# A planner in the kernel sets every engine's order; the first two batches' softmax works on the allowed columns only

## The chip, the core and the metric

The kernel runs on one NeuronCore of a Trainium2 chip. Five engines work side by side, each through its own queue in order: TensorE (PE, with PEld for its weight loads), VectorE (DVE), ScalarE (ACT), GpSimd (POOL) and SyncE (SP), which here issues all transfers between HBM and the on-chip memory. The metric is the time of one execution in microseconds (us), less is better; the time shown is the median of three runs.

## What is computed

```python
# q, k, v: (8 batches, 8 heads, 576 positions, 64) float32
scores = q @ k.T / 8                          # per batch and head
mask_local   = (rel >= 0) & (rel < 32)        # heads 0..3;  rel = query - key
mask_strided = (rel >= 0) & (key % 32 == query % 32)   # heads 4..7
attn = softmax(where(mask, scores, -1e9));  y = attn @ v
x = y as (4608 tokens, 512)
h = x @ w_in                                  # 512 -> 2048, weights in float64
g = h * clip(h + 3, 0, 6) / 6
out = g @ w_out                               # 2048 -> 512
```

Each query sees at most 32 keys (local heads) or 18 keys (strided heads).

## The kernel before

**Attention.** The unit is a pair of heads, 4 pairs per batch, 32 in all; pairs 0 and 1 of a batch are local, 2 and 3 strided. A pair's steps (`pair_steps`, L265) are: load q and k (L240, four DMAs each, 72 KB per DMA) and v (L251, L258, L262); turn q and k by DVE transposes (L289, L293, L301); scores on PE (`s_step`, L320); softmax (`softmax`, L196); turn the probabilities (`p_blocks`, L366, DVE; or `p_whole`, L392, PE and a copy, for the first five pairs); the product with v (`v_step`, L402, tile pv); and the two halves of x, high part by ACT (L428) and rest by DVE (L429). A head is cut into 6 blocks of 96 queries by 128 keys (local) or 5 of 126 by 126 (strided), so a block holds far more columns than its queries may see. Scores of pairs 0 to 7 (batches 0 and 1) are one float32 product (L333); from pair 8 on q and k are each split in a high and a rest part and the product runs in fp32r (L335). Softmax takes the blocks one by one: mask and row minimum in one DVE instruction with its accumulator read (L206), exponent and sum in one ACT instruction with its accumulator read (L211), the division on POOL (L361).

**FFN.** 512 tokens of a batch are one pass of 16 chunks (fc). Per chunk: 12 matmuls of 128x512 into ph (L512 to L514, three per 128 rows of x: weights and x are both in two fp32r parts); then a chain of four instructions, relu on ACT (L539), gate on DVE (L540), high part gh on ACT and rest gl on POOL (L101, L102); then 12 matmuls into four acc banks, two with gh and one with gl (L495, L496, L497). The last 64 positions of each batch are collected over four batches and make a pass of 256 tokens (phl, accl), run after batches 2 and 7.

**Weights.** 32 parts of 512 KB come as float64 bit patterns (L115). A conversion (`conv`, L117) takes three ACT, two DVE (L124, L126) and one POOL instruction per part.

**The order.** While the FFN of batch b runs, the attention of batch b + 1 is issued between its chunks. The first two batches follow a hand-written string ORDER; the later ones a fixed sequence spread over the chunks. The tile framework's scheduler then moves instructions on each engine by its own simulated times and priorities. The first two chunks of batch 0 are started early, 128 rows of x at a time (`mm1_early`, L516).

Of the kernel before, what the change touches and what calls it, by code (L numbers as in the profile page):

```python
# [1 line left out]

# [8 lines left out]
I32 = mybir.dt.int32  # L11
# [10 lines left out]
QB = 96  # L22
NPOS = 18
# [4 lines left out]
WA = 6  # L28
NB = 3
VB = 1  # L30
PLAIN = 8
EC = 2
KP = 4
HP = 100
EV = 11
EARLY = 5
ORDER = "l w q0 t0 q1 v0 t1 a0 b0 v1 q2 l a1 v2 b1 q3 p0 t2 o0 l a2 b2 p1 t3 o1 l a3 v3 w l b3 p2 o2 w q4 w m0 p3 l m1 m2 o3 m3 v4 | q5 t4 a4 b4 v5 t5 q6 p4 o4 a5 l q7 b5 t6 p5 o5 a6 b6 q8 v6 p6 v7 o6 t7 a7 b7 t8 p7 l q9 o7 v8 v9"
DENSE = 8
RATE = 0.95
UB = 3  # L40
AHEAD = 6
# [3 lines left out]
def attention_ffn(ctx: ExitStack, tc, q, k, v, w_in, w_out, out):  # L45
# [7 lines left out]
    LEFT = S - TOK  # L53
    SCALE = 1.0 / float(D) ** 0.5

    const = ctx.enter_context(tc.tile_pool(name="const", bufs=1))
    wp = ctx.enter_context(tc.tile_pool(name="wp", bufs=1))
    xp = ctx.enter_context(tc.tile_pool(name="xp", bufs=2))
    gp = ctx.enter_context(tc.tile_pool(name="gp", bufs=2))
    up = ctx.enter_context(tc.tile_pool(name="up", bufs=UB))  # L60
    ap = ctx.enter_context(tc.tile_pool(name="ap", bufs=1))
    sp = ctx.enter_context(tc.tile_pool(name="sp", bufs=3))
    pacc = ctx.enter_context(tc.tile_pool(name="pacc", bufs=1, space=PSUM))
    pwk = ctx.enter_context(tc.tile_pool(name="pwk", bufs=4, space=PSUM))


    ident = const.tile([P, P], F32, name="ident")
    make_identity(nc, ident)
    three = const.tile([P, 1], F32, name="three")
    nc.vector.memset(three, 3.0)  # L70


    mloc = const.tile([QB, P], F32, name="mloc")
    nc.gpsimd.memset(mloc, 0.0)
    nc.gpsimd.affine_select(
        out=mloc, in_=mloc, compare_op=ALU.is_ge, fill=NEG,
        base=PAD, pattern=[[-1, P]], channel_multiplier=1)
    nc.gpsimd.affine_select(
        out=mloc, in_=mloc, compare_op=ALU.is_ge, fill=NEG,
        base=STRIDE - 1 - PAD, pattern=[[1, P]], channel_multiplier=-1)  # L80
    mstr = const.tile([SB, SB], F32, name="mstr")
    nc.gpsimd.memset(mstr, 0.0)
    mstr3 = mstr.rearrange("p (r m) -> p r m", r=RB)
    nc.gpsimd.affine_select(
        out=mstr3, in_=mstr3, compare_op=ALU.is_ge, fill=NEG,
        base=0, pattern=[[-NPOS, RB], [-1, NPOS]], channel_multiplier=1)
    nc.gpsimd.affine_select(
        out=mstr3, in_=mstr3, compare_op=ALU.is_ge, fill=NEG,
        base=NPOS - 1, pattern=[[NPOS, RB], [0, NPOS]], channel_multiplier=-1)
# [3 lines left out]

    NQ = 4
    FQ = NFC // NQ
    wts = {}

    def split(src, hi, lo, eng):  # L100
        nc.scalar.copy(hi, src)  # L101
        eng.tensor_tensor(out=lo, in0=src, in1=hi.bitcast(F32), op=ALU.subtract)  # L102

    def weight_steps():

        parts = [(w, g, i) for g in range(NQ) for w in "io" for i in range(4)]
        raws = {}

        def load(w, g, i):
# [4 lines left out]
            t = raws[w, g, i] = wp.tile([P, TOK, 2], I32, tag=f"w{w}{g}{i}", name=f"raw{w}{g}{i}")  # L114
            nc.sync.dma_start(t, src.bitcast(I32).rearrange("p (n t) -> p n t", t=2))  # L115

        def conv(w, g, i):  # L117
            raw = raws[w, g, i]
            f = up.tile([P, TOK], I32, tag="u", name=f"f{w}{g}{i}")
            r = raw.rearrange("p n t -> p (n t)")[:, :TOK]  # L120
            nc.scalar.activation(f.bitcast(F32), raw[:, :, 1].bitcast(F32), AF.Copy, scale=2.0 ** -112)
# [501 lines left out]
```

## Time and profile before

| | us |
|---|---|
| median of three runs (lowest, highest) | 1003.33 (1002.16, 1006.83) |
| the profiled execution | 1004.04 |
| its span, first to last instruction | 1002.3 |
| PE busy in it | 950.4 (95%) |
| DVE, ACT, POOL busy | 623.8, 507.1, 408.1 |
| HBM read, written | 46.84 MB, 9.44 MB |
| mean granted TensorE clock | 0.975 of full |

The span falls into stages by the matmuls: attention of batch 0 and the first FFN chunks up to 66.3 us (the first acc matmul), FFN of batch 0 beside attention of batch 1 up to 178.7, six stages of one FFN pass beside one batch of attention, the short pass for the left-over tokens at 389.8 to 439.9, FFN of batch 7 with no attention beside it, and a second short pass at the end. A busy PE is not PE at its peak: matmuls overlap, and when the granted clock is 0.5 each takes twice as long.

### The profile page before, as it was taken

The page shows a single profiled execution, that of the slowest core. Times are in us where ns is not written, and L with a number is a line of the kernel's source. Part 1 is how long each engine was busy: PE and PEld are TensorE (multiplying, and loading weights), DVE is VectorE, ACT ScalarE, POOL GpSimd, SP SyncE. Part 2 cuts the span into 40 slices and gives each one's busy share as a digit, 9 for nine tenths or more (in the row PEclk, how much of TensorE's full clock was granted, in tenths as well). Part 3 has the DMA queues.
Part 4 walks back from the last instruction along what each step waited for, and adds up shares of the span by engine and source line. Part 5 has one row for each costly group of instructions (what it writes and reads, how often), then busy time and mean ns, then how long its engine had stood idle before and what let it go on. Part 6 is the DMA issues. An engine that isn't in the chain of part 4 may idle for free. (4 is left out here: it accounts for less than half of the span.)

```text
span 1002.3 us, 14999 instructions
## 1 busy us (share of the span) xinstructions
PE 950.4 (95%) x4848; PEld 767.8 (77%) x4848; DVE 623.8 (62%) x1837; ACT 507.1 (51%) x1378; POOL 408.1 (41%) x381
## 2 busy tenths in 40 slices
PE   5789897999999999999999999999899999999997
PEld 4667675887787778988787777777778888788896
DVE  7677988677767775136877767776766766211111
ACT  5778676545555534345454544464455544322232
POOL 4446656443444434234443433443344433222221
PEclk8799997999999999999999999999899999999999
DMA  7699601212132222002222211222213110100010
GB/s 150 148 282 281 137 13 27 67 31 47 26 81 39 37 37 61 22 19 43 37 38 60 61 33 35 46 67 39 37 26 81 31 22 14 43 1 1 1 43 21
DMA packets 207085, 57.25 MB, mean 57 GB/s; under 512 B 198304, under 2 KB 198304, under 8 KB 207008
## 3 DMA queue, kind: packets, MB, share of 16 engines
q1 hardware_dynamic: 207008, 56.31, 24.9%
q8 instruction: 38, 0.62, 0.3%
q14 instruction: 39, 0.32, 0.1%
HBM read 46.84 MB, written 9.44 MB: 56 GB/s over the span
## 5 line engine op out<-in xcount | busy, mean ns | idle before, releaser
L102 POOL TENSOR_TENSOR gl<-u,gh 128x512 fp32r<-128x512 f32 x128 | 168.5, 1318 | 255.7 <-ACT gh L101 226.9
L512 PE MATMUL ph<-xh,wi 128*128 128x512 f32 x512 | 207.1, 405 | 5.9 <-ACT wi L101 4.0
L495 PE MATMUL acc<-wo,gh 128*128 128x512 f32 x512 | 203.1, 397 | 1.2 <-ACT gh L101 1.1
L513 PE MATMUL ph<-xl,wi 128*128 128x512 f32 x512 | 203.2, 397 | 0.1
L514 PE MATMUL ph<-xh,wi 128*128 128x512 f32 x512 | 202.1, 396 | 0.0
L496 PE MATMUL acc<-wo,gh 128*128 128x512 f32 x512 | 201.3, 393 | 0.0
L211 ACT ACTIVATE e<-e,st 126x126 f32<-126x126 f32 (+2 forms) x352 | 137.3, 392 | 79.0 <-DVE st L206 77.4
L101 ACT CAST gh<-u 128x512 fp32r<-128x512 f32 x128 | 79.2, 619 | 163.6 <-DVE u L540 143.2
L497 PE MATMUL acc<-wo,gl 128*128 128x512 f32 x512 | 161.0, 397 | 0.0
L540 DVE SCALAR_TENSOR_TENSOR u<-u,ph 128x512 f32<-128x512 f32 x128 | 86.4, 675 | 104.9 <-ACT u L539 104.1
L361 POOL TENSOR_TENSOR e<-e,st 96x96 f32<-96x96 f32 (+1 forms) x96 | 92.9, 981 | 116.7 <-DVE st L358 94.3
L539 ACT ACTIVATE u<-ph,three 128x512 f32<-128x512 f32 x128 | 87.2, 682 | 92.8 <-PE ph L514 88.1
L512 PEld LDWEIGHTS ph<-xh,wi 128*128 128x128 f32 x512 | 97.3, 190 | 31.5 <-ACT wi L101 5.0
L514 PEld LDWEIGHTS ph<-xh,wi 128*128 128x128 f32 x512 | 97.8, 191 | 21.9 <-issue 0.2
L495 PEld LDWEIGHTS acc<-wo,gh 128*128 128x128 f32 x512 | 96.8, 189 | 22.4 <-ACT gh L101 2.2
L513 PEld LDWEIGHTS ph<-xl,wi 128*128 128x128 f32 x512 | 97.8, 191 | 18.5 <-DVE xl L429 0.6
L497 PEld LDWEIGHTS acc<-wo,gl 128*128 128x128 f32 x512 | 95.9, 190 | 20.5 <-issue 0.2
L496 PEld LDWEIGHTS acc<-wo,gh 128*128 128x128 f32 x512 | 96.7, 189 | 18.2
L386 DVE STREAM_TRANSPOSE atstr<-e 32x160 f32<-32x160 f32 x196 | 65.6, 335 | 10.7 <-POOL e L361 8.1
L386 DVE STREAM_TRANSPOSE atloc<-e 32x160 f32<-32x160 f32 (+1 forms) x156 | 56.6, 363 | 16.3 <-POOL e L361 14.3
L206 DVE CUSTOM_DVE_ANT_0 e<-ps,e 96x128 f32<-96x128 f32 (+2 forms) x264 | 65.0, 280 | 2.3
L211 ACT ACTIVATION_READ_ACCUMULATOR e<-e,st 96x1 f32 (+1 forms) x352 | 66.2, 188 | 0.0
(176 smaller groups left out, 1359.1 us busy)
## 6 DMA issues: line engine op xcount, KB each, us to landing
qn<-in_q_dram SPq DMA_DIRECT2D x128, 72.0 KB
kn<-in_k_dram SPq DMA_DIRECT2D x128, 72.0 KB
rawi<-in_moe_w_in_dram SPq DMA_DIRECT2D x16, 512.0 KB
rawo<-in_moe_w_out_dram SPq DMA_DIRECT2D x16, 512.0 KB
out_dram<-ob SPq DMA_DIRECT2D x32, 256.0 KB
vt<-in_v_dram SPq DMA_DIRECT2D x32, 160.0 KB
vt<-in_v_dram SPq DMA_DIRECT2D x160, 31.5 KB
out_dram<-obl SPq DMA_DIRECT2D x8, 128.0 KB
```

The lines of the kernel that those rows point to most:

```text
L102: eng.tensor_tensor(out=lo, in0=src, in1=hi.bitcast(F32), op=ALU.subtract)
L211: nc.scalar.activation(e[:, u, c], e[:, u, c], AF.Exp, bias=mn[:, u:u + 1], scale=-1.0, accum_out=sm[:, u:u + 1])
L361: nc.gpsimd.tensor_tensor(out=x, in0=x, in1=sm[:, bl].unsqueeze(2).to_broadcast(x.shape), op=ALU.mult)
L386: nc.vector.transpose(at[ks, i0:, qs], e[qs, i0:, ks])
L495: nc.tensor.matmul(acc[i], gh[:, sl], woh, start=fc == 0, stop=False)
L496: nc.tensor.matmul(acc[i], gh[:, sl], wol, start=False, stop=False)
L497: nc.tensor.matmul(acc[i], gl[:, sl], woh, start=False, stop=last)
L512: nc.tensor.matmul(ph, wih, xh[:, c], start=c == 0, stop=False)
L513: nc.tensor.matmul(ph, wih, xl[:, c], start=False, stop=False)
L514: nc.tensor.matmul(ph, wil, xh[:, c], start=False, stop=c == NCC - 1)
L539: nc.scalar.activation(u, ph, AF.Relu, bias=three)
L540: nc.vector.scalar_tensor_tensor(out=u, in0=u, scalar=6.0, in1=ph, op0=ALU.min, op1=ALU.mult)
```

## The change

The kernel is written anew around a list planner in it (`Plan`). Every step is an `op` with an engine (or a choice of two), a duration written in the code, what it reads and writes, and a due time; PSUM banks are slots that an op takes and gives back. `emit` walks a simulated time: of the ops whose inputs are there it takes the one that can start first, by due time where several can, and at the end writes all ops in order of their planned start. The framework's scheduler is off (`manual_schedule`), so this is each engine's order. What is computed stays the same. The parts:

- **Batches 0 and 1** (`kept_pair`): scores stay one float32 product, local heads in the same 6 blocks, strided heads in 8 blocks of 128 by 72. ACT copies only the columns that a query may see (64 of 128 for local, 18 of 72 for strided) out of PSUM, in 3 or 4 strips of 32 rows per four blocks. Then, once per head: mask on POOL, maximum on DVE, subtraction on POOL, exponent on ACT, sum on DVE, reciprocal on DVE, product on POOL. All probabilities are turned by DVE (6 strips of 32x192 per local head, 4 of 32x256 per strided head); the PE transposes and their copies go.
- **From batch 2 on** (`pair`): the same instructions as before, whole blocks and split scores, with pv of a pair in one run.
- **PSUM**: four acc banks, two ph banks and two score banks, instead of four acc and four shared. The output tiles use x's memory.
- **Weights**: relu with a slope (Prelu) keeps the sign in the first ACT instruction, so that one DVE instruction (join) takes the place of two.
- **Order of pairs** 0, 2, 1, 3 (and 2, 3, 0, 1 in batch 1).

```diff
-EC = 2
-ORDER = "l w q0 t0 q1 v0 t1 a0 b0 v1 q2 l a1 v2 b1 q3 p0 t2 o0 l a2 b2 p1 t3 o1 l a3 v3 w l b3 p2 o2 w q4 w m0 p3 l m1 m2 o3 m3 v4 | q5 t4 a4 b4 v5 t5 q6 p4 o4 a5 l q7 b5 t6 p5 o5 a6 b6 q8 v6 p6 v7 o6 t7 a7 b7 t8 p7 l q9 o7 v8 v9"
+AHEAD = 27.0
+T0 = 50.0
+TILE = 101.0
+HOP = 0.12
+FETCH = 2.2
...
+    def emit(self):
...
+                    t = max(t0, avail[n])
...
+                    if first is None or (t, due, n) < first:
+                        first = (t, due, n)
...
+            free[e] = end = t + (us() if callable(us) else us)
+            if after:
+                end = dma = max(end + FETCH, dma) + after
...
+        for _, _, n, e in sorted(order):
...
-        def conv(w, g, i):
...
-            nc.vector.scalar_tensor_tensor(out=r, in0=f, scalar=3, in1=r,
...
-            nc.vector.scalar_tensor_tensor(out=f, in0=f, scalar=-2147483648, in1=r,
...
+        def high():
+            f = new(xp, fkey, [P, TOK], I32, f"f{name}")
+            nc.scalar.activation(f.bitcast(F32), tiles[key][:, :, 1].bitcast(F32), AF.Prelu, scale=2.0 ** -112, alpha=2.0 ** 32)
...
+        def join():
+            f = tiles[fkey]
+            nc.vector.scalar_tensor_tensor(out=f, in0=f, scalar=3, in1=bits(),
                                            op0=ALU.logical_shift_left, op1=ALU.bitwise_or)
...
+        op("SP", 0.1, load, writes=[key], due=-2 + 0.1 * k if k < 16 else due - 20.0, early=7.0 if k < 16 else due - 30.0, after=1.7)
+        op("ACT", 0.68, high, reads=[key], writes=[fkey], due=due - 5, room=LATE)
+        op("ACT", 0.68, low, writes=[key], due=due - 5)
+        op("DVE", 0.95, join, reads=[key], writes=[fkey], due=due - 3)
+        op("ACT", 0.63, hi, reads=[fkey], writes=[key], due=due - 2)
+        op("POOL", 1.4, lo, reads=[fkey, key], writes=[key + ("lo",), key], due=due - 1)
...
-    def softmax(ps, mask, skip, e, mn, sm):
...
-            nc.vector.tensor_tensor_reduce(
-                out=e[:, u, c], in0=ps[:, u, 0, c], in1=m[:, u, c], scale=-SCALE, scalar=BIG,
...
-            nc.scalar.activation(e[:, u, c], e[:, u, c], AF.Exp, bias=mn[:, u:u + 1], scale=-1.0,
...
+    def timing(g):
+        b = g // NPAIR
+        if not b:
+            return T0 - 6.0 * (NPAIR - g)
+        return wanted[b] - 6.0 - (NPAIR - 1 - g % NPAIR) * (wanted[b] - opens[b]) / NPAIR
...
+    def kept_pair(g):
+        b, c = divmod(g, NPAIR)
+        c = TURNS[b][c]
...
+            op("SP", 0.25, load, writes=[nkey], due=-60 + 2 * g + (x == "k") if early else due - 35, early=0 if early else due - 45, after=1.9)
...
+                rows = v[b, h0 + j].rearrange("(m t i) d -> i m t d", t=8, i=4)
+                for i in range(4):
+                    nc.sync.dma_start(tiles[vkey][PAD * i:PAD * i + NPOS, j], rows[i])
+        op("SP", 0.2 if loc else 0.4, load_v, writes=[vkey], due=-59.5 + 2 * g if early else due - 30, early=0 if early else due - 35, after=1.7)
...
+                        if e == "ACT":
+                            nc.scalar.copy(to, src)
...
+            def masked(j=j):
...
+                    nc.gpsimd.tensor_tensor(out=e_of(j), in0=e_of(j), in1=m.unsqueeze(1).to_broadcast([n, nblk, w]), op=ALU.add)
...
+                nc.vector.tensor_reduce(out=st_of(j, 0), in_=e_of(j), axis=AX.X, op=ALU.max)
...
+                nc.gpsimd.tensor_tensor(out=x, in0=x, in1=st_of(j, 0).unsqueeze(2).to_broadcast(x.shape), op=ALU.subtract)
...
+                nc.scalar.activation(e_of(j), e_of(j), AF.Exp, scale=SCALE)
...
+                nc.vector.tensor_reduce(out=st_of(j, 1), in_=e_of(j), axis=AX.X, op=ALU.add)
...
+                nc.gpsimd.tensor_tensor(out=x, in0=x, in1=st_of(j, 1).unsqueeze(2).to_broadcast(x.shape), op=ALU.mult)
...
+                op("DVE", 6 * 0.37 if loc else 4 * 0.435, tr, reads=[ekeys[j]], writes=[akeys[j]], due=due - 2 + j)
...
+    def pair(g):
...
+            op("SP", 0.25, load, writes=[nkey], due=due - 38, early=due - 45, after=1.9)
...
-        if b * NPAIR + c >= EARLY:
-            pv = [p_blocks(0), p_blocks(1)] + [v_step(g) for g in groups]
...
-    def mm1_early(c):
-        for fc in range(EC):
-            if c == 0:
-                early[fc] = pwk.tile([P, TOK], F32, tag="w", name=f"ph0_{fc}")
-            mm1(early[fc], fc, c, *xs[0])
...
+                    nc.tensor.matmul(acc, gh, woh, start=fc == 0, stop=False)
+                    nc.tensor.matmul(acc, gh, wol, start=False, stop=False)
+                    nc.tensor.matmul(acc, gl, woh, start=False, stop=end)
+                op("PE", 0.683, mm, reads=list(gk) + wkeys, writes=[("acc", i)],
+                   due=s0 + (fc + 1.5 + i * 0.12) * chunk, mode="f")
...
+                op("PE", 0.683 if n == TOK else 0.36, mm1, reads=xkeys(c) + wkeys, writes=[pk],
+                   due=s0 + (fc + c * 0.12) * chunk, mode="f")
...
+    with tc.manual_schedule():
+        plan.emit()
```

**SP, the start of the program, before.** In a name such as qn0_2 the digits are batch and pair; rawi and rawo are weight parts (group and part). The queue begins so:

```order
L115 DMA rawi00_109<-in_moe_w_in_dram 128x1024
L240 DMA qn0_0_119<-in_q_dram 32x18x32 x4
L240 DMA kn0_0_124<-in_k_dram 32x18x32 x4
L240 DMA qn0_1_139<-in_q_dram 32x18x32 x4
L240 DMA kn0_1_144<-in_k_dram 32x18x32 x4
L251 DMA vt0_0_149<-in_v_dram 96x2x64
L258 DMA vt0_0_149<-in_v_dram 128x5x64 x2
L251 DMA vt0_1_213<-in_v_dram 96x2x64
L258 DMA vt0_1_213<-in_v_dram 128x5x64 x2
L240 DMA qn0_2_218<-in_q_dram 32x18x32 x4
```

And now, from the eighth row on (the first seven are the q and k of pairs 0, 2, 1 and the q of pair 3):

```order
L343 DMA kn0_3_172<-in_k_dram 32x18x32 x4
L347 DMA v0_0_163<-in_v_dram 96x2x64
L352 DMA v0_0_163<-in_v_dram 128x5x64 x2
L460 DMA v0_2_182<-in_v_dram 18x8x64 x8
L347 DMA v0_1_186<-in_v_dram 96x2x64
L352 DMA v0_1_186<-in_v_dram 128x5x64 x2
L460 DMA v0_3_190<-in_v_dram 18x8x64 x8
L273 DMA rawi00_237<-in_moe_w_in_dram 128x1024
L273 DMA rawi01_239<-in_moe_w_in_dram 128x1024
```

The first weight part has moved from row 1 to row 15, behind all q, k and v of batch 0; 15 more weight parts follow it, and then q, k and v of pair 2 of batch 1, which before came behind five weight parts (pair 0 there).

**DVE, ahead of the first gate, before.** st is a head's sums, fo and rawo a weight part, xl the rest of x, u the FFN's gate; pv0_30 is batch 0, pair 3:

```order
L124 SCALAR_TENSOR_TENSOR rawo02_657<-fo02_699,rawo02_657 128x512
L429 TENSOR_TENSOR xl0_108<-pv0_30_605,xh0_107 128x28x16
L429 TENSOR_TENSOR xl0_108<-pv0_34_637,xh0_107 128x4x16
L126 SCALAR_TENSOR_TENSOR fo02_699<-fo02_699,rawo02_657 128x512
L206 ISA e1_01_778,st1_01_780<-ps1_014_815,mloc_89 96x128
```

And now, rows 69 to 79 of DVE (row 84 is the last part of x of pair 3, rows 86 and 87 turn q and k of pair 3 of batch 1, row 88 is the first gate):

```order
L584 STREAM_TRANSPOSE atkept_188<-e0_93 32x8x32 x4
L550 TENSOR_REDUCE st0_3_509<-e1_110 128x8
L440 STREAM_TRANSPOSE qt1_2_349<-qn1_2_373 128x18x32
L553 TENSOR_SCALAR st0_3_509<-st0_3_509 128x8
L554 RECIPROCAL st0_3_509<-st0_3_509 128x8
L381 TENSOR_TENSOR x0_11_678<-pv0_10_623,x0_10_677 128x512
L381 TENSOR_TENSOR left1_1_80<-pv0_11_624,left0_1_79 128x64
L584 STREAM_TRANSPOSE atkept_188<-e1_110 32x8x32 x4
L440 STREAM_TRANSPOSE kplain_118<-kn1_2_383 128x18x32
L289 SCALAR_TENSOR_TENSOR fo03_646<-fo03_646,rawo03_256 128x512
L289 SCALAR_TENSOR_TENSOR fi10_663<-fi10_663,rawi10_258 128x512
```

The transposes of batch 1's pair 2, which need transfers that stand behind 16 weight parts on SP, now stand ahead of the x of batch 0's pairs 1 and 3.

**PE, FFN of batch 7, before.** acc7_0 is acc bank 0 of batch 7, gh7_6 and gl7_6 the two parts of chunk 6:

```order
L513 MATMUL ph7_8_8590<-xl7_7354,wi21_1157 128x512
L495 MATMUL acc7_0_8362<-wo12_1027,gh7_6_8540 128x512
L496 MATMUL acc7_0_8362<-wo12_1027,gh7_6_8540 128x512
L495 MATMUL acc7_1_8363<-wo12_1027,gh7_6_8540 128x512
L496 MATMUL acc7_1_8363<-wo12_1027,gh7_6_8540 128x512
L495 MATMUL acc7_2_8364<-wo12_1027,gh7_6_8540 128x512
L496 MATMUL acc7_2_8364<-wo12_1027,gh7_6_8540 128x512
L497 MATMUL acc7_0_8362<-wo12_1027,gl7_6_8541 128x512
L497 MATMUL acc7_1_8363<-wo12_1027,gl7_6_8541 128x512
```

And now:

```order
L877 MATMUL acc7_0_8384<-wo13_1132,gh7_7_8592 128x512
L878 MATMUL acc7_0_8384<-wo13_1132,gh7_7_8592 128x512
L879 MATMUL acc7_0_8384<-wo13_1132,gl7_7_8597 128x512
L920 MATMUL ph7_8_8567<-x7_30_8189,wi23_1233 128x512
L921 MATMUL ph7_8_8567<-x7_31_8190,wi23_1233 128x512
L922 MATMUL ph7_8_8567<-x7_30_8189,wi23_1233 128x512
L877 MATMUL acc7_1_8390<-wo13_1132,gh7_7_8592 128x512
```

The rest part gl is now needed by the third matmul of a chunk and not the seventh. From the last ph matmul of a chunk to the first acc matmul that needs its gh, PE has 29 other matmuls in the list before (chunk 7) and 18 now (chunk 8).

More of the change, by code (lines that the diff above doesn't have):

```diff
@@ L1 @@
+import heapq
 from contextlib import ExitStack
+from functools import partial
 import concourse.bass as bass
@@ L98, in attention_ffn, with identity @@
[L98 to L109, printed above, removed]
+    left = [[[const.tile([P, HALF * LEFT], F32R, name=f"left{i}_{c}") for i in range(2)]]
+            for c in range(NCC)]
+    def identity():
+        nc.vector.memset(three, 3.0)
+        make_identity(nc, new(const, ("ident",), [P, P], F32, "ident"))
```

1126 lines of the change are left out of this document (704 added, 422 removed).

## The prediction

> **What bounds the kernel now.** I read the page first: the busy time of TensorE, the rows of 40 slices (25.06 us each) for PE, its granted clock and the transfer rate.
>
> ```profile
> PE 950.4 (95%) x4848; PEld 767.8 (77%) x4848; DVE 623.8 (62%) x1837; ACT 507.1 (51%) x1378; POOL 408.1 (41%) x381
> PE   5789897999999999999999999999899999999997
> PEclk8799997999999999999999999999899999999999
> GB/s 150 148 282 281 137 13 27 67 31 47 26 81 39 37 37 61 22 19 43 37 38 60 61 33 35 46 67 39 37 26 81 31 22 14 43 1 1 1 43 21
> ```
>
> PE is the bound: 950.4 of 1002.3 us. What isn't 9 lies in the first seven slices; there the weights come in (282 GB/s in slices 3 and 4). So I cut the span into stages at the matmuls that begin each FFN pass. Columns: window, its us, busy us (instructions) of PE, PEld, DVE, ACT, POOL, granted clock, DMA share, GB/s.
>
> ```profile
> 0.00:66.30 66.30, 48.20 (x296) 38.27 (x296) 47.51 (x182) 47.01 (x166) 29.72 (x52) 0.87 0.79 176
> 66.30:178.70 112.40, 100.33 (x469) 74.17 (x470) 95.79 (x210) 79.29 (x185) 69.73 (x57) 0.92 0.50 130
> 178.70:389.80 211.10, 204.25 (x1017) 164.08 (x1016) 153.92 (x464) 108.16 (x304) 90.34 (x76) 0.99 0.22 45
> 389.80:439.90 50.10, 50.10 (x322) 44.90 (x321) 7.85 (x19) 17.18 (x39) 12.53 (x17) 1.00 0.09 30
> 439.90:754.40 314.50, 305.36 (x1518) 245.46 (x1517) 229.84 (x699) 161.60 (x457) 132.41 (x113) 0.98 0.22 44
> 754.40:857.10 102.70, 102.70 (x521) 82.67 (x520) 67.80 (x226) 51.70 (x149) 40.52 (x36) 1.00 0.15 34
> 857.10:945.50 88.40, 88.40 (x401) 73.07 (x401) 12.49 (x20) 24.14 (x40) 20.59 (x16) 1.00 0.03 12
> 945.50:1002.30 56.80, 51.05 (x313) 45.18 (x312) 8.55 (x19) 18.04 (x39) 12.28 (x16) 0.97 0.09 28
> ```
>
> Three things stand here. The opening takes 66.3 us before the first acc matmul. The second stage has 12.1 us without PE and a clock of 0.92. The six stages of one FFN pass and one batch of attention (windows three, five and six) take 211.1 + 314.5 + 102.7 = 628.3, 104.7 each, while the best of them takes 102.7 with PE never idle. Batch 7 without attention takes 88.4, so attention costs a good stage 14.3.
>
> For the opening I asked what PE waits for (us in total, times, longest), and when the first gate and the first acc matmul come (third field: first and last start).
>
> ```profile
> PE ps L333 <- DVE kplain L293: 9.7, 2, 9.1
> L540 DVE SCALAR_TENSOR_TENSOR u<-u,ph x128: 636/684/691, 63.3 to 946.5; 128x512 f32<-128x512 f32 x128
> L495 PE MATMUL acc<-wo,gh x512: 387/389/796, 66.3 to 952.1; 128*128 128x512 f32 x171
> ```
>
> PE starts on the first q and k, and the first chunk ends with the gate at 63.3; acc follows 3.0 later.
>
> **The opening: transfers.** SP's timeline (start, duration), and the window in which transfers were fastest:
>
> ```profile
> 1.20 2.04 SPq L240 DMA_DIRECT2D qn<-in_q_dram  x4
> 3.28 2.92 SPq L240 DMA_DIRECT2D kn<-in_k_dram  x4
> 10.57 0.50 SPq L251 DMA_DIRECT2D vt<-in_v_dram  x1
> 11.11 1.02 SPq L258 DMA_DIRECT2D vt<-in_v_dram  x2
> 19.36 8.19 SPq L262 DMA_DIRECT2D vt<-in_v_dram  x10
> 78.00:86.00 8.00, 7.76 (x41) 5.72 (x39) 6.84 (x9) 6.37 (x12) 4.42 (x4) 1.00 0.99 372
> ```
>
> Now eight groups of q and k go first: SP is busy with one for 2.04 to 2.92, say 2.25, so 18 us from 1.2 on. Then four v: two local at 0.50 + 1.02, two strided of eight DMAs at 0.82 (8.19 for ten), together 16.2; a DMA now moves less, and at 0.65 (an estimate between the 0.50 of L251 and 0.82) it is 13.4. The weights begin at 32.6. Sixteen parts of 512 KB at the page's 282 GB/s take 1.86 each, 29.8 in all; at the best rate of the trace, 372 GB/s with the DMA engines 99% busy, 22.5. So q of batch 1's pair 2, the next in line, lands between 55 and 62, and k behind it: 56 to 64.
>
> **The opening: DVE.** Its rows by shape (busy, mean ns, then idle before):
>
> ```profile
> L289 DVE STREAM_TRANSPOSE qplain<-qn 128x576 f32<-128x576 f32 x8 | 8.1, 1014 | 2.6 <-DMA qn<-in_q_dram 2.6
> L386 DVE STREAM_TRANSPOSE atloc<-e 32x192 f32<-32x192 f32 x130 | 48.1, 370 | 2.0
> L124 DVE SCALAR_TENSOR_TENSOR rawi<-fi,rawi 128x512 int32<-128x512 int32 x16 | 12.0, 751 | 8.4 <-ACT rawi L122 8.3
> L126 DVE SCALAR_TENSOR_TENSOR fi<-fi,rawi 128x512 int32<-128x512 int32 x16 | 17.0, 1061 | 0.3
> L202 DVE TENSOR_TENSOR e<-ps,mloc 96x256 f32<-96x256 f32 x72 | 29.0, 418 | 32.2 <-PE ps L335 31.4
> L357 DVE TENSOR_SCALAR st<-st 96x6 f32<-96x6 f32 x32 | 13.3, 414 | 5.0 <-ACT e L211 4.7
> L358 DVE RECIPROCAL st<-st 96x6 f32<-96x6 f32 x32 | 5.6, 174 | 0.5
> L429 DVE TENSOR_TENSOR xl<-pv,xh 128x448 fp32r<-128x448 f32 x16 | 16.2, 1013 | 18.7 <-ACT xh L428 18.5
> ```
>
> Ahead of the first gate DVE now has: 8 turns of q and k at 1.01 (8.1), 24 local turns at 0.370 (8.9), 16 strided ones a third wider, 0.49 as an estimate (7.9), 11 joins at 0.75 (8.3), 16 reduces, which the trace does not have, by the nearest row 0.42 (6.7; from 0.17 to 1.01 each), 8 sums and reciprocals at 0.59 (4.7), four rests of x at 1.16 by L429's length (4.6), and four turns of batch 1's q and k at 1.01 (4.0): 53 us of 72. DVE's sum alone doesn't set the time, but its order does: the turns of batch 1's pair 2 stand ahead of the x of pairs 1 and 3, so x, ph and the gate wait for a transfer behind sixteen weights. Landing at 62, two turns (2), then 8 of joins, turns and x that stand between: first gate 72 (70 to 74; with fast transfers 65), first acc 75. The same wait holds up the four instructions of each chunk behind it. So the opening is about 9 longer, although it loses all probability transposes on PE.
>
> **Second stage.** Its 112.4 are 12.1 idle and 100.3 busy at clock 0.92, so 92.3 at full clock. Since the softmax works on six tenths fewer columns (384 and 144 per head instead of 768 and 630), I take half of the idle away (bounds: all, none) and give the clock back, as slow clocks stand in the first slices only, next to idle ones. The extra score and pv blocks (8 instead of 5 per strided head, 24 matmuls) cost nothing by streamed columns and 4.1 by this row's busy time (0.17 each); I take 1.5.
>
> ```profile
> L333 PE MATMUL ps<-kplain,qplain 64*126 64x126 f32 x40 | 6.7, 292 | 0.9 <-DVE st L206 0.9
> ```
>
> 92.3 + 1.5 + 6 = 99.8. Batch 1 then begins at 75 + 99.8 = 174.8 against 178.7: −3.9. Bounds: 160 (fast transfers, no idle) and 190 (a clock of 0.92 and all idle kept).
>
> **The joins.** One DVE instruction replaces two per part, some 1.0 less of DVE for each of 32 parts, on no path after batch 0. What it costs beside POOL:
>
> ```profile
> 105.93 3.63 DVE L126 SCALAR_TENSOR_TENSOR fi<-fi,rawi 128x512 int32<-128x512 int32 x1
> 106.49 1.27 POOL L102 TENSOR_TENSOR wi<-fi,wi 128x512 fp32r<-128x512 f32 x1
> 107.72 1.28 POOL L102 TENSOR_TENSOR gl<-u,gh 128x512 fp32r<-128x512 f32 x1
> ```
>
> A join that starts while POOL goes from one instruction to the next took 3.63, not 0.75. [...] With L126's mean of 1.06 instead of 0.75 the eleven joins cost 3.4 more and the sum would be 980.
>
> **Six stages.** Matmuls are the same, FFN and attention. The planner has PE's work in one list, with pv of a pair in one run, where before its matmuls came in pieces between FFN groups:
>
> ```profile
> 754.40:857.10 102.70, 7.43 (x88) 5.66 (x88) 1.00 0.15 34
> 857.10:945.50 88.40, 1.20 (x16) 1.05 (x16) 1.00 0.03 12
> ```
>
> These are L412's matmuls in the best stage and in batch 7, 84 and 75 ns each. Grouping saves between nothing and about 3.2; I take 1.7, a quarter of the 7.43. So 101.0 per stage, bounds 99.5 and 104.7 (no better than the mean before): 6 x 101 = 606, −22.3. ACT, DVE and POOL are 39 to 73% busy in these stages, so their work stays under PE. The short passes (50.1, 56.8) and batch 7 (88.4) have the same work and hardly any idle: nothing.
>
> **Sum.** 1004.04 − 3.9 − 22.3 = 977.8 for an execution like the profiled one; that lies 0.7 above the median, so 977.
>
> **Rivals.** *B: the opening as short as planned.* If SP's issues and the weights overlap better than my chain (372 GB/s and no turn held up), the first acc comes at about 59, batch 1 at 159, −16 more: 961. For it: the DMA share is 0.79 in the opening, not 1. Against: one queue, 20 us of it for q and k.
>
> *C: the stages don't shrink.* The planner's durations are constants; an engine that runs late against them makes PE wait in queue order, with no other work to take. The gain of 22.3 then fails: 999. For it: 2.7 of an average stage before were idle, waits that the new order needn't remove.
>
> *D: slower.* PE's list now leaves 18 matmuls (4.1 us) from a chunk's last ph to the first acc that needs it, 29 (6.7 us) before, and wants gl two matmuls after gh, six before. The chain is
>
> ```profile
> L539 ACT ACTIVATE u<-ph,three 128x512 f32<-128x512 f32 x128 | 87.2, 682 | 92.8 <-PE ph L514 88.1
> L540 DVE SCALAR_TENSOR_TENSOR u<-u,ph 128x512 f32<-128x512 f32 x128 | 86.4, 675 | 104.9 <-ACT u L539 104.1
> L101 ACT CAST gh<-u 128x512 fp32r<-128x512 f32 x128 | 79.2, 619 | 163.6 <-DVE u L540 143.2
> L102 POOL TENSOR_TENSOR gl<-u,gh 128x512 fp32r<-128x512 f32 x128 | 168.5, 1318 | 255.7 <-ACT gh L101 226.9
> L361 POOL TENSOR_TENSOR e<-e,st 96x640 f32<-96x640 f32 x32 | 41.0, 1282 | 0.0
> ```
>
> 0.682 + 0.675 + 0.619 + 1.318 = 3.29 up to gl, and 20 matmuls at 0.230 (88.4 over 16 x 24) are 4.6, so 1.3 is left, 3.8 before; a softmax product of 1.28 on POOL just ahead of gl, or an attention instruction on ACT or DVE, is enough to stop PE. There are 16 x 7 = 112 such chunks. A stop of 0.24 per chunk on average eats the 26 of gain; at 0.4, 1022. Against it: the planner knows these lengths and places the softmax where the chain leaves room.
>
> *E: POOL holds the joins.* Eleven joins ahead of the first gate, next to POOL's mask, subtract and product passes (three per head now, against one), at 2 us instead of 0.75 (between 0.75 and 3.63) cost 13.8 more. Batch 1 begins at 188: 1004.04 + 9.9 − 22.3, 991. The row of 3.63 speaks for it, the mean of 0.75 against. [...]
>
> **How the numbers follow.** The forecast has a chance of 0.52, B 0.14, C 0.10, D 0.11, E 0.13. This kernel can be told from no change at about 0.5%, 5 us: faster is below 998.3, slower above 1008.3. Faster: forecast 0.50, B 0.14, E 0.11, C 0.03, in all 0.78. No change: forecast 0.02, E 0.02, C 0.06, D 0.02, 0.12. Slower: C 0.01, D 0.09, 0.10. The range takes in C at 999 and half a stage's doubt around it, up to 1003, and goes down to both unknowns at their low end (batch 1 at 160, stages of 99.5: 1004 − 18.7 − 31.3, 954), 955; what it leaves out is D and little of C.
>
> **What would show it.** Right: first gate at 70 to 74 behind a DVE turn of batch 1 that waits for its transfer; batch 1 at about 175; stages of 101 with PE at 100%; short passes unchanged. Wrong: first acc below 62 (B), stages of 104 or more (C), waits of acc for gl or gh in the hundreds (D), joins with a mean of 2 us in the opening (E).

## The result and the profile after

The changed kernel takes 971.98 us (median of four runs, 971.58 to 972.17); the kernel before takes 1004.55 in the same series, the ratio is 0.968, 95% interval 0.965 to 0.970. The forecast was 977, range 955 to 1003. The profiled execution took 971.58 with a span of 969.8, 32.5 less than the span before.

The page's first rows:

```profile
PE 926.3 (96%) x4952; PEld 762.8 (79%) x4952; DVE 604.1 (62%) x1651; ACT 524.2 (54%) x1330; POOL 429.2 (44%) x420
PE   5489999999999999999999999999999999999997
PEclk9978999999999999999999999999999999999999
GB/s 119 235 201 205 141 112 17 84 26 53 35 66 56 45 38 52 45 22 67 17 38 25 82 41 39 41 82 41 39 41 68 56 14 1 44 1 0 21 25 22
```

PE's gaps are gone everywhere but in the first three slices and the last. The clock row needs care: the trace has no record of the clock before 56.2 us, and the 9 of the first two slices only says that none is there. The spacing of the matmuls shows half clock from the first one at 8.3 up to 56.2 (0.43 between the starts of equal ones, 0.23 at full clock; the last section has the lines). So the 0.90 in the first line below is too high: of the opening's 84.9 us, 56.2 (with the 8.3 ahead of the first matmul), 10.3 and 6.8 count as half clock, which leaves 0.57. In the kernel before the same holds only up to 12.7 us, 3.6 after its first matmul.

The stages, cut at the same matmuls as before (first acc, first ph of batch 1, first ph of batch 7; columns as in the prediction):

```profile
0.00:84.90 84.90, 53.90 (x301) 44.58 (x302) 59.75 (x128) 49.36 (x134) 44.03 (x77) 0.90 0.67 180
84.90:177.70 92.80, 92.64 (x498) 73.43 (x497) 62.39 (x116) 67.70 (x143) 62.90 (x61) 1.00 0.38 104
177.70:826.30 648.60, 641.60 (x3464) 527.94 (x3463) 462.42 (x1373) 366.63 (x978) 289.31 (x251) 1.00 0.22 45
826.30:911.30 85.00, 85.00 (x376) 70.38 (x375) 11.01 (x16) 23.14 (x36) 19.55 (x16) 1.00 0.03 13
```

The third line answers to this one of before, six stages and the short pass between them:

```profile
178.70:857.10 678.40, 662.40 (x3373) 537.11 (x3372) 459.42 (x1407) 338.64 (x949) 275.80 (x242) 0.99 0.20 42
```

The two first stages together became 1.0 shorter (178.7 to 177.7; forecast 3.9): the opening is 18.6 longer and the second stage 19.6 shorter, with hardly any idle and a full clock. The six stages with the short pass became 29.8 shorter (forecast 22.3), and what follows them 1.7 (145.2 to 143.5; forecast nothing). In the six stages PE's idle time went from 16.0 (678.40 − 662.40) to 7.0.

The opening shows a wait that the kernel before did not have. ScalarE and VectorE of the changed kernel (start, duration, in brackets the idle time before it):

```profile
38.43 0.66 ACT L281 ACTIVATE fi<-rawi 128x512 f32<-128x512 f32 x1 [10.03 <-DMA rawi<-in_moe_w_in_dram]
40.63 0.90 DVE L289 SCALAR_TENSOR_TENSOR fi<-fi,rawi 128x512 int32<-128x512 int32 x1 [9.29 <-ACT rawi L285]
63.59 1.19 DVE L440 STREAM_TRANSPOSE qt<-qn 128x576 f32<-128x576 f32 x1
77.38 0.68 DVE L932 SCALAR_TENSOR_TENSOR u<-u,ph 128x512 f32<-128x512 f32 x1
```

ScalarE stood 10.0 on the first weight part with softmax copies queued behind it; VectorE stood 9.3 behind ScalarE. The turn of batch 1's q, which the prediction named as the wait, began at 63.59 with no wait at all; the first gate came at 77.4, not 72. From 63.4 to 84.9 the chain that ended last runs through PE, but for 2.2 us, and 13.3 of these 21.5 us are at half clock (up to 69.9, and 76.7 to 83.5). At the spacing of full clock, 0.23 instead of 0.43, that would be some 6 less (an estimate from these rows). The first weight was late because of what the prediction summed up on SP:

```profile
19.63 6.71 SPq L460 DMA_DIRECT2D v<-in_v_dram  x8
28.02 6.44 SPq L460 DMA_DIRECT2D v<-in_v_dram  x8
34.50 1.89 SPq L273 DMA_DIRECT2D rawi<-in_moe_w_in_dram  x4
```

The weights began at 34.5 (forecast 32.6).

### The profile page after: what moved, and what is told of

It is laid out like the page before. It is cut to its first block, busy times and chain, and to the rows that moved or that the text cites. A ratio compares the mean times of both kernels' runs of the same rounds, so it can differ in the third digit from the quotient of the medians.

```text
span 969.8 us, 15040 instructions
## 1 busy us (share of the span) xinstructions
PE 926.3 (96%) x4952; PEld 762.8 (79%) x4952; DVE 604.1 (62%) x1651; ACT 524.2 (54%) x1330; POOL 429.2 (44%) x420
## 4 chain that ended last, share of the span: by engine, by line
PE 77%; DVE 10%; ACT 4%; issue 3%; SPq 3%; DMA 2%; POOL 1%; POOLq 0%; DVEq 0%; ACTq 0%
PE ph L920 11%; PE ph L921 10%; PE ph L922 10%; PE acc L877 10%; PE acc L879 10%; PE acc L878 10%; PE ps L755 3%; PE phl L920 1%; PE phl L922 1%; PE phl L921 1%; DVE atloc L811 1%; PE accl L879 1%; SPq L343 1%; PE accl L877 1%; PE accl L878 1%
## 5 line engine op out<-in xcount | busy, mean ns | idle before, releaser
L920 PE MATMUL ph<-x,wi 128*128 128x512 f32 x512 | 204.8, 400 | 1.2 <-ACT left L378 1.1
L921 PE MATMUL ph<-x,wi 128*128 128x512 f32 x512 | 202.1, 395 | 0.2 <-DVE x L381 0.2
L922 PE MATMUL ph<-x,wi 128*128 128x512 f32 x512 | 201.8, 394 | 0.0
L879 PE MATMUL acc<-wo,gl 128*128 128x512 f32 x512 | 200.0, 391 | 0.3 <-POOL gl L941 0.2
L779 ACT ACTIVATE e<-e,st 126x126 f32<-126x126 f32 (+2 forms) x264 | 102.9, 391 | 45.2 <-DVE st L773 44.6
L936 ACT CAST gh<-u 128x512 fp32r<-128x512 f32 x128 | 79.4, 620 | 65.9 <-DVE u L932 60.2
L920 PEld LDWEIGHTS ph<-x,wi 128*128 128x128 f32 x512 | 97.2, 190 | 21.1 <-ACT left L378 1.2
L922 PEld LDWEIGHTS ph<-x,wi 128*128 128x128 f32 x512 | 97.2, 190 | 21.1
L921 PEld LDWEIGHTS ph<-x,wi 128*128 128x128 f32 x512 | 97.3, 190 | 17.2 <-DVE x L381 0.9
L878 PEld LDWEIGHTS acc<-wo,gh 128*128 128x128 f32 x512 | 96.2, 188 | 17.7
L794 POOL TENSOR_TENSOR e<-e,st 96x96 f32<-96x96 f32 (+1 forms) x72 | 71.1, 1002 | 41.5 <-DVE st L789 35.5
L773 DVE CUSTOM_DVE_ANT_0 e<-ps,e 126x126 f32<-126x126 f32 (+2 forms) x264 | 65.2, 279 | 2.8
L811 DVE STREAM_TRANSPOSE atstr<-e 32x160 f32<-32x160 f32 x168 | 56.3, 335 | 8.3 <-POOL e L794 5.2
L755 PEld LDWEIGHTS ps<-ksplit,qq 128*96 128x96 f32 (+1 forms) x264 | 43.7, 173 | 20.2 <-DVE x L381 3.8
L755 PE MATMUL ps<-ksplit,qq 128*96 128x256 f32 (+1 forms) x264 | 53.5, 284 | 5.3 <-DVE x L381 2.4
```

The lines of the kernel that those rows point to most:

```text
L755: nc.tensor.matmul(view()[:, u], tiles["qq"][:, j, q0[i]:q0[i] + n], keys(tiles["kk"], pad)[:, j, :, kc], start=True, stop=True)
L779: nc.scalar.activation(e, e, AF.Exp, bias=st_of(j, 0)[:, i:i + 1], scale=-1.0, accum_out=st_of(j, 1)[:, i:i + 1])
L878: nc.tensor.matmul(acc, gh, wol, start=False, stop=False)
L879: nc.tensor.matmul(acc, gl, woh, start=False, stop=end)
L920: nc.tensor.matmul(ph, wih, xh, start=c == 0, stop=False)
L921: nc.tensor.matmul(ph, wih, xl, start=False, stop=False)
```

## The experiments

Each kernel is the changed kernel with the edit shown, or with several of them; 971.98 is the time to compare with. Where the start of batch 1's FFN is given, it is its first ph matmul in the profiled execution (177.7 in the changed kernel).

**Weights later on ScalarE.** The planner believes that the first sixteen parts can be taken up 12 us later.

```diff
-        op("ACT", 0.68, high, reads=[key], writes=[fkey], due=due - 5, room=LATE)
+        op("ACT", 0.68, high, reads=[key], writes=[fkey], due=due - 5, room=LATE + (12.0 if k < 16 else 0.0))
```

> Only the planner's belief changes when the first sixteen weight parts can be taken up (12 us later), so that on ScalarE the copies of pairs 1 and part of pair 3 stand ahead of the first weight instruction; the transfers keep their order. Blocked-queue theory: the 10.0 us that ScalarE waited for the first weight, with softmax copies queued behind it, made the opening long; the first acc matmul comes at 75 to 78 instead of 84.9 and the time is 963 to 966. Late-weights theory: the weights land at the same time as before, and their conversion sets the end of the opening; first acc at 82 or later, time 969 to 973.

Measured: 989.8, outside both expectations. The 10.0 wait on ScalarE is gone, but the next one comes to light:

```profile
60.24 1.15 DVE L440 STREAM_TRANSPOSE qt<-qn 128x576 f32<-128x576 f32 x1 [3.54 <-DMA qn<-in_q_dram]
61.25 1.79 DVE L584 STREAM_TRANSPOSE atkept<-e 32x256 f32<-32x256 f32 x4
64.17 0.60 ACT L378 CAST x<-pv 128x256 fp32r<-128x256 f32 x1 [8.84 <-PE pv L636]
```

VectorE waits for batch 1's q behind sixteen weights, as the prediction said; the strided probabilities (L584) stand behind it, and ScalarE waits 8.8 for the product with v that comes of them. Two stretches at half clock follow, behind the half clock up to 56.5:

```profile
60.00:80.00 20.00, 16.27 (x64) 12.97 (x65) 11.27 (x17) 8.43 (x24) 3.50 (x4) 0.58 0.43 77
104.00:118.00 14.00, 14.00 (x47) 10.49 (x45) 4.84 (x11) 8.41 (x25) 5.90 (x8) 0.51 0.68 180
```

Together they cost about 16.27 x 0.42 + 14.00 x 0.49 = 13.7 of PE's time (those of the changed kernel behind 56.2, shown at the end, some 7), and batch 1's FFN begins at 192.1.

**The same, with batch 1's q and k ahead of eight weight parts.** Only the place of these eight DMAs on SP is new against the kernel just shown.

```diff
-            op("SP", 0.25, load, writes=[nkey], due=-60 + 2 * g + (x == "k") if early else due - 35, early=0 if early else due - 45, after=1.9)
+            op("SP", 0.25, load, writes=[nkey], due=-60 + 2 * g + (x == "k") if early else -1.25 if g == 4 else due - 35, early=0 if early else 7.0 if g == 4 else due - 45, after=1.9)
```

> act_later, with q and k of batch 1's first pair loaded behind eight weight parts instead of sixteen. Theory that act_later lost its time to the second wait of the opening (the DVE turn of that q stood 3.5 on its transfer with the strided x behind it, ScalarE then 8.8): the turn no longer waits, the FFN of batch 1 begins at 175 to 182 instead of 192, time 970 to 979. Rival, the loss lies in the planned order or in the half-clock stretches whatever the turn does: 985 to 991.

Measured: 968.96, batch 1's FFN at 178.1. The turn still waits, 5.6, but it now stands at 49.50 instead of 60.24, and 14.0 of batch 1's start came back. Behind the half clock at the start, here up to 62.7, only one stretch is left, 96.8 to 103.6. This speaks for the second wait, with the half clock that follows it, as the loss of the kernel above; what share is the wait's and what the clock's was not told apart. But batch 1's FFN begins no earlier than in the changed kernel (177.7), where ScalarE waited 10.0. So the blocked queue alone is not what the opening costs: with the weights still landing at 38, what is taken off ScalarE's wait comes back elsewhere; where was not followed further.

**Weights first.** Four weight parts go ahead of the strided v transfers on SP.

```diff
-        op("SP", 0.2 if loc else 0.4, load_v, writes=[vkey], due=-59.5 + 2 * g if early else due - 30, early=0 if early else due - 35, after=1.7)
+        op("SP", 0.2 if loc else 0.4, load_v, writes=[vkey], due=(-59.5 + 2 * g if loc else -1.65) if early else due - 30, early=(0 if loc else 7.05) if early else due - 35, after=1.7)
```

> On SP the first four weight parts go ahead of the sixteen strided v transfers (13.2 us of SP). The first weight lands at about 25 instead of 38.4. Blocked-queue theory and late-weights theory alike: first acc at 72 to 76, time 960 to 964. Rival, the work on ScalarE and VectorE from 38 to 77 us is the bound of the opening: first acc at 81 or later, time 968 to 972.

Measured: 962.84, the time as expected, but by another way: the first acc came at 80.4, near the rival's 81 and not at 72 to 76, and batch 1's FFN at 175.8, only 1.9 earlier. Most of the gain lies later: from there to batch 7 it took 641.8 instead of 648.6, and why is not shown. ScalarE's wait shrank to 4.0:

```profile
27.26 0.66 ACT L281 ACTIVATE fi<-rawi 128x512 f32<-128x512 f32 x1 [4.00 <-DMA rawi<-in_moe_w_in_dram]
```

**Weights first, and batch 1's q and k early** (both edits shown above).

> weights_first with the same earlier load; there the turn of that q waited 2.4 and that of k 1.1. If these waits still hold the end of the opening: 957 to 961. If they are covered by then: 962 to 964.

Measured: 959.94 (958.41 and 961.47), ratio to the kernel before 0.955, interval 0.951 to 0.960; batch 1's FFN at 170.1. The time is the one expected for two separate waits, but the trace does not show them as that. The waits of 2.4 and 1.1 that the expectation names were those of the next pair, whose transfers the edit leaves in place, and its q still waits 2.3 (at 69.53); the turn whose transfer was moved had no wait with the weights first alone (at 60.58). Against that kernel batch 1's FFN begins 5.7 earlier, with 57.8 instead of 69.0 us of half clock in the opening, and the six stages take 4.4 more (646.2 for 641.8). So what the edit gains is a new order and a clock that comes back sooner; which of the two was not told apart, and the 2.9 between the medians is no more than the 3.1 between the two runs here. This is the fastest version found; it beats both kernels.

**The planner knows SP's durations.**

```diff
-            op("SP", 0.25, load, writes=[nkey], ...
+            op("SP", 2.16, load, writes=[nkey], ...
-        op("SP", 0.2 if loc else 0.4, load_v, writes=[vkey], ...
+        op("SP", 1.6 if loc else 6.6, load_v, writes=[vkey], ...
-            op("SP", 0.25, load, writes=[nkey], due=due - 38, ...
+            op("SP", 2.16, load, writes=[nkey], due=due - 38, ...
-        op("SP", 0.3 if loc else 0.6, load_v, ...
+        op("SP", 1.6 if loc else 8.2, load_v, ...
-        op("SP", 0.1, load, writes=[key], ...
+        op("SP", 0.5, load, writes=[key], ...
```

> The planner's SP durations become those of the trace (2.16 for a group of q or k, 1.6 and 6.6 for v, 8.2 for ten v transfers, 0.5 for a weight part), everywhere. Blocked-queue theory: the planner itself now places the weights behind the softmax copies, first acc at 75 to 78, the six stages as they were, time 963 to 967. Rival: with SP planned as a scarce queue the loads of the later stages move too and cost as much as is gained, time 970 or more.

Measured: 964.92, in the expected range, by another way. The first acc came at 69.8, 15.1 earlier, but the second stage took 109.3 instead of 92.8, with half clock from 100.2 to 113.9. So batch 1's FFN begins at 179.1, no earlier; the six stages take 639.6 instead of 648.6. What the wrong SP durations cost shows in the stages, where PE's idle time falls from 7.0 to 3.1.

**Durations and weights first together.**

> Measured SP durations in the planner and the first four weight parts ahead of the strided v transfers. Theory that the two gains are of different kinds (first weight at 25 in place of 38; loads of the later stages planned in time): 954 to 960. Rival, both remove the same wait: 962 to 966.

Measured: 962.72, the rival's value: the two gains do not add up. The first acc came at 75.2. Six stages 640.1, batch 1's FFN at 177.4.

**All three edits.**

> Measured SP durations, four weight parts first and the earlier load together. If the waits of the opening add up: 955 to 960. If the opening is now set by the work of ScalarE and VectorE: 961 to 964.

Measured: 964.13; no gain. Batch 1's FFN begins at 164.4, 13 earlier than without the early q, but the next stage takes 109.2 instead of 99.8 and the rest 545.5 instead of 540.3:

```profile
72.10:164.40 92.30, 92.30 (x498) 73.47 (x497) 60.51 (x110) 69.65 (x151) 65.96 (x64) 1.00 0.43 121
164.40:273.60 109.20, 104.16 (x539) 83.27 (x538) 85.38 (x241) 60.47 (x163) 54.55 (x47) 0.97 0.25 50
```

The stage has 5.0 idle (0.2 without the early q) and a clock of 0.97, which together are 8 of the 9.4; why the rest is slower is open. In the first line, too, the clock was at half up to 63.0, as the matmuls' spacing shows.

**pv in pieces.** From batch 2 on a pair's product with v is cut into four ops with FFN matmuls between them.

```diff
...
-        op("PE", 2.2 if loc else 1.8, mm, reads=akeys + [("vt",)], writes=[*vb, *xk, lk], take=vb, due=due - 1001, room=ROOM, mode="v")
+        for n0 in range(PIECES):
+            op("PE", (2.2 if loc else 1.8) / PIECES, partial(mm, n0), reads=akeys + [("vt",)], writes=[*vb, *xk, lk], take=vb if n0 == 0 else None, due=due - 1001,
+               room=0.3 if n0 else ROOM, mode="v")
```

> From batch 2 on each pair's product with v is cut into four pieces with FFN matmuls between them (96 visits instead of 24); the planner plans it so. Grouping theory: each visit costs PE some 0.2 us (f to pv 0.318 instead of 0.227, pv to f 0.15 instead of 0.08 by the starts in the trace), 72 more visits cost 14, time 984 to 988. Rival, the gain of the six stages came from fewer waits alone: 971 to 975.

Measured: 998.30 (998.17 to 999.17), 26.3 more, above the expectation of 12 to 16 more; the six stages take 674.4 instead of 648.6, and batch 1 begins 0.9 later. One visit of the cut kernel in PE's timeline:

```profile
243.22 0.39 PE L936 MATMUL ph<-x,wi 128*128 128x512 f32 x1
243.54 0.44 PE L842 MATMUL pv<-atstr,vt 126*64 126x126 f32 x4
243.90 0.50 PE L891 MATMUL acc<-wo,gh 128*128 128x512 f32 x1
244.24 0.39 PE L892 MATMUL acc<-wo,gh 128*128 128x512 f32 x1
244.47 0.40 PE L893 MATMUL acc<-wo,gl 128*128 128x512 f32 x1
```

From one start to the next a dense FFN matmul takes 0.23 (244.24 to 244.47). The one ahead of pv takes 0.32 (243.22 to 243.54) and the one behind it 0.34 (243.90 to 244.24): the price of 0.2 that the expectation named had left the second out. The two add 0.20 to a visit, and the 0.07 that the expectation counts from pv to the next matmul makes 0.27; where the rest up to 26.3 / 72 = 0.37 is spent these rows do not show.

**pv in halves** (PIECES = 2).

> As pv_pieces but two pieces per pair, 24 more visits to pv instead of 72. If each visit has its own price (26.3 over 72 is 0.37): 979 to 983. If the cost came from holding the two score banks longer rather than from the visits, it goes with the length of a pair's pv and not with the count: 985 to 995, or 972 to 975 where two pieces leave the banks as they were.

Measured: 981.27, 9.3 more. With 24 more visits that is 0.39 each, with 72 it was 0.37: the price goes by the visit, as expected.

**Batch 1 as from batch 2 on.**

```diff
-KEPT = 8
+KEPT = 4
...
-    for g in range(6):
+    for g in range(4):
...
-        for g in range(max(6, (b + 1) * NPAIR), (b + 2) * NPAIR):
+        for g in range((b + 1) * NPAIR, (b + 2) * NPAIR):
...
-                                                     ("kk", 0), ("kk", 1), ("qq", 0), ("qq", 1)], due=wanted[1] - 10)
-                op("POOL", 0.8, masks_str, writes=[("ident",)], due=wanted[1] - 9)
+                                                     ("kk", 0), ("kk", 1), ("qq", 0), ("qq", 1)], due=T0 - 6)
+                op("POOL", 0.8, masks_str, writes=[("ident",)], due=T0 - 5)
```

> Batch 1 gets the whole-block softmax and split scores of the later batches; only batch 0 keeps plain scores and allowed columns. Theory that the allowed columns pay in the second stage, where the weight conversions run beside the softmax: the second stage becomes DVE- and ACT-bound (about 100 us of each by batch 2's softmax plus the conversions) and 8 to 15 longer, time 980 to 987. Rival, the planner's order alone made that stage short: 969 to 975.

Measured: 994.37, 22.4 more; the direction was right, the size too small. Its second stage and the one after it:

```profile
81.70:191.80 110.10, 93.56 (x434) 72.84 (x433) 89.55 (x232) 82.08 (x202) 70.80 (x55) 0.92 0.32 87
191.80:308.30 116.50, 108.67 (x578) 87.66 (x577) 93.53 (x279) 72.03 (x196) 55.47 (x49) 0.97 0.25 51
```

No engine is full (DVE 81%), so it is not a bound of DVE or ACT as expected. The second stage is 17.3 longer and has 16.5 of idle. PE waits now for one of them and now for another (both stages, up to 305):

```profile
PE acc L878 <- POOL wo L298: 6.8, 3, 2.9
PE ps L755 <- POOL ksplit L700: 4.7, 2, 4.5
PE ps L755 <- DVE left L381: 3.8, 2, 1.9
PE acc L877 <- ACT wo L294: 3.1, 3, 1.6
```

The waits are for converted weights (wo) and for split keys and the work around them, and the clock falls to 0.92; that the two get in each other's way is a reading of these rows and was not tried. The next stage is 15.4 longer (101.1 in the changed kernel), and 3.2 of the opening and 6.0 of the stages behind come back. So the softmax on allowed columns with plain scores is worth about 22 in batch 1, next to the weights. Whether the columns or the missing split carries it was not told apart.

**Two joins again.**

```diff
-            nc.scalar.activation(f.bitcast(F32), tiles[key][:, :, 1].bitcast(F32), AF.Prelu, scale=2.0 ** -112, alpha=2.0 ** 32)
+            nc.scalar.activation(f.bitcast(F32), tiles[key][:, :, 1].bitcast(F32), AF.Copy, scale=2.0 ** -112)
...
-            nc.vector.scalar_tensor_tensor(out=f, in0=f, scalar=3, in1=bits(),
+            nc.vector.scalar_tensor_tensor(out=bits(), in0=f, scalar=3, in1=bits(),
                                            op0=ALU.logical_shift_left, op1=ALU.bitwise_or)
+            nc.vector.scalar_tensor_tensor(out=f, in0=f, scalar=-2147483648, in1=bits(),
+                                           op0=ALU.bitwise_and, op1=ALU.bitwise_or)
```

> The weight conversion gets its second DVE instruction back, the planner's durations stay. If DVE is as tight as its 85% from 40 to 60 us says, eleven more instructions of 0.7 to 1 ahead of the first gate push the FFN of batch 0 by 3 to 8: 975 to 980. Rival, DVE has room there since ScalarE and the transfers set the pace: 971 to 974.

Measured: 993.16, 21.2 more, far above both.

```profile
0.00:95.40 95.40, 55.93 (x300) 47.05 (x301) 71.10 (x140) 49.46 (x134) 44.69 (x77) 0.93 0.69 188
95.40:199.90 104.50, 98.07 (x498) 76.75 (x497) 80.09 (x135) 67.46 (x143) 64.77 (x60) 0.95 0.25 67
199.90:848.60 648.70, 641.87 (x3465) 527.99 (x3464) 463.00 (x1375) 366.57 (x978) 289.91 (x253) 1.00 0.22 45
```

In the opening DVE has 71.1 instead of 59.75 to do, 11.4 more, and the opening is 10.5 longer; in the second stage 17.7 more, and it is 11.7 longer. The six stages are the same to 0.1. So while weights were converted here, more work on DVE made the stage longer, nearly one for one in the opening and two thirds in the second stage. How much of it is DVE's time itself is not told apart: half clock lasts longer too, up to 74.5 in the opening (by the matmuls; the 0.93 is too high), and in the second stage, at a clock of 0.95, PE is busy 5.4 longer and idle 6.3 longer.

**gl twice.** POOL computes gl of every chunk a second time into the same tile.

```diff
+                eng.tensor_tensor(out=g, in0=tiles[uk][:, :n], in1=tiles[gk[0]][:, :n].bitcast(F32), op=ALU.subtract)
                 eng.tensor_tensor(out=g, in0=tiles[uk][:, :n], in1=tiles[gk[0]][:, :n].bitcast(F32), op=ALU.subtract)
```

> POOL computes gl twice for every chunk, 1.32 longer, nothing else changes. Slack theory: in the trace the end of gl lies a median of 1.53 ahead of its first matmul and under 1.32 in 41 of 112 chunks; the missing pieces add up to 22, so 985 to 1000. Theory that PE has other work to take in (the queue is fixed, but a stop in one chunk gives the next one room): 972 to 980. If slower than 1010, the softmax products queued behind gl on POOL are hit too.

Measured: 1022.74, 50.8 more, ratio to the kernel before 1.020 (1.017 to 1.023). PE's first wait by size, and the pass of batch 7:

```profile
PE acc L879 <- POOL gl L942: 22.2, 40, 2.0
865.30:959.60 94.30, 88.64 (x376) 69.29 (x375) 11.01 (x16) 23.12 (x36) 38.83 (x31) 1.00 0.03 12
```

The stops are those that the expectation summed (22 in 41 chunks). But each costs more than it shows: in batch 7, where no attention runs beside it, the pass is 9.3 longer (94.3 for 85.0) and only 5.7 of it is idle. Of the rest of the 50.8, 33.0 lie in the six stages (681.6 for 648.6), 6.0 ahead of them and 2.7 in the short pass at the end; how it divides there between stops, what follows them and POOL's queue was not told apart.

## Why the prediction was right, and where it was not

The sign, the place of most of the gain (the six stages) and the sum were right; the sum was 5 high. That it came so near is in part luck: the opening came out 9.9 longer than forecast, the second stage 7.0 shorter, the six stages 7.5 and what follows 1.7.

- **SP's chain**: weights at 34.5 for 32.6, q of batch 1 at 60.2 in the kernel where its turn waits for it, forecast 55 to 62. Right.
- **The opening**: the step that failed is "x, ph and the gate wait for a transfer behind sixteen weights". In the changed kernel an earlier wait, ScalarE's on the first weight, had taken its place. The one named is real but hidden behind it: it came to light in the kernel with later weights on ScalarE (3.5, with 8.8 on ScalarE behind it), and 14.0 came back when its transfer was moved. The gate came at 77.4 for 72, and from gate to acc it took 7.5, where the prediction had the 3.0 of the kernel before; PE was busy there and at half clock from 76.7 to 83.5. So the first acc came at 84.9 for 75. The prediction has no term for ScalarE's wait and none for the clock of the opening. Moving both transfers gave 12 (971.98 to 959.94), 7.6 of it by the start of batch 1's FFN.
- **DVE's sum in the opening** "alone doesn't set the time": failed, as far as one kernel shows it. The second join back cost 21.2, 11.7 of it in the second stage, where the prediction had the saving "on no path after batch 0".
- **The second stage**: 92.8 for 99.8. Half of the idle was kept in the forecast; all of it went, and the clock came back in full. The kernel with batch 1 as in the later stages has it at 110.1, so that term belongs to the new softmax (its columns or its plain scores) and not to the list alone. The misses of the two stages nearly cancel, 177.7 for 174.8, which is luck.
- **The six stages**: −29.8 for −22.3. The term for grouped pv, 6 x 1.7 = 10.2, was right in size, if the price measured above held in the kernel before: the traces show 54 visits of PE to pv before and 25 after, at 0.37 each 10.7. The prediction's own working gives 11.1 (a quarter of 7.43 is 1.86, not 1.7). Most of the rest are terms that it left out: idle time fell by 9.0, and a mean clock of 0.99 for 1.00 over 662 is some 6.
- **D** was real and near: gl ended a median of 1.5 ahead of its first matmul in the trace (forecast 1.3; the 3.8 that the prediction gives for the list before should be 4.8, 35 matmuls at 0.230 less 3.29), and 1.32 more on POOL turns the gain of 32 into a loss of 18. That it did not happen fits the durations in the planner (0.69, 0.68, 0.63, 1.35), which are close to the measured ones (0.69, 0.68, 0.62, 1.32); a plan with wrong ones was not tried. **E** did not happen: the eleven joins ahead of the first gate took 0.79 on average, seven of them 0.65 to 0.68 and four 0.90 to 1.30.

## What to carry to other kernels

Ask which waits stand in series: in an opening where each queue is in order, taking away the first can bring out the second. Making room on the one queue that showed the wait cost 17.8; bringing the transfers forward gained 9.1 and, with both, 12. A list planner is as good as its durations: the ones of the compute chain were right and held a tight order, the ones of the DMA queue were five to sixteen times too short, and mending them gained 7. A clock row counts as full clock where the trace has no record (up to 56.2 here); the spacing of equal matmuls, 0.43 or 0.23 here, tells the clock there too. Count how often TensorE changes between kinds of small and large matmuls: grouping is a gain (0.37 to 0.39 a visit here) that no idle time shows.

## What the runs showed of the hardware

- A visit of TensorE to a few small matmuls (pv, 64 to 126 columns) between large ones (128x512) cost 0.37 to 0.39 in the time of the kernel: the large one ahead of it takes 0.32 and the one behind it 0.34, start to start, instead of 0.23; the rest is not located.
- The clock. In the changed kernel's opening (window, its length, PE busy, clock, DMA share, GB/s):

```profile
40.00:56.20 16.20, 15.13 (x79) 1.00 1.02 411
56.20:59.60 3.40, 1.91 (x31) 1.00 0.82 190
59.60:69.90 10.30, 7.00 (x35) 0.50 0.33 62
69.90:76.70 6.80, 5.54 (x46) 1.00 0.59 100
76.70:83.50 6.80, 6.80 (x22) 0.50 0.53 146
```

The 1.00 of the first line is no reading, since the clock's records begin at 56.2. Equal matmuls tell it by their starts, ahead of 56.2, in a recorded stretch of half clock, and at full clock:

```profile
53.40 0.63 PE L922 MATMUL ph<-x,wi 128*128 128x512 f32 x1
53.83 0.63 PE L920 MATMUL ph<-x,wi 128*128 128x512 f32 x1
67.61 0.63 PE L921 MATMUL ph<-x,wi 128*128 128x512 f32 x1
68.04 0.63 PE L922 MATMUL ph<-x,wi 128*128 128x512 f32 x1
84.41 0.39 PE L921 MATMUL ph<-x,wi 128*128 128x512 f32 x1
84.64 0.39 PE L922 MATMUL ph<-x,wi 128*128 128x512 f32 x1
```

From start to start it is 0.43, 0.43 and 0.23, so at half clock 1.9 times as long, not quite twice. The kernel before begins in this way too, at half clock until its records begin with full clock at 12.7 (equal score matmuls start 0.21 apart ahead of that and 0.11 apart from there on), and the one with two joins up to 74.5. Behind the start, half clock came in stretches of 10.3 and 6.8 in the changed kernel, and of 3.4 (seven times), 10.2 and 13.7 in the kernel before, leaving out the one that the end of the span cuts off in each. The stretch from 59.6 stands behind 3.4 us in which PE was idle for 1.5; the longest gap, 60.1 to 63.4, comes when half clock has begun. PE was busy for all of 76.7 to 83.5, and for all 14.0 us from 104 to 118 in the kernel with later weights on ScalarE, at half clock (0.50 and 0.51). What sets off a stretch here, and what ends it, was not tried.
- Of the changed kernel's 32 joins (two inputs, 128x512), 15 started with POOL idle and took 0.64 to 0.69. Of the 17 that started while POOL ran an instruction, the 14 with 0.21 or more of it left ended 0.55 after that instruction, as here, with 0.77 of gl left; the other three, with at most 0.10 left, took 0.67 to 0.69. The longest took 1.78, behind 1.23 of POOL's; the 3.63 of the kernel before did not come again.

```profile
169.19 1.30 POOL L941 TENSOR_TENSOR gl<-u,gh 128x512 fp32r<-128x512 f32 x1 [0.66 <-POOL e L544]
169.72 1.32 DVE L289 SCALAR_TENSOR_TENSOR fo<-fo,rawo 128x512 int32<-128x512 int32 x1 [1.32 <-ACT rawo L285]
```

- The stops of TensorE cost more than their idle time in the pass of batch 7 with gl twice: 9.3 for 5.7, at full clock (1.00).
